# Sparse attention and an ELU feed-forward: staging loads on two queues, halves and pairs of loads, and a new written order

## The chip, the cores and the metric

The kernel runs on one core of a Trainium2 chip. The metric is the device time of one execution in microseconds (us). The kernel before takes 312.54 us (median of 3 runs, 312.42 to 312.94). The core's engines are TensorE (PE, matrix multiplication), VectorE (DVE), ScalarE (ACT, also `exp` and `ln`), GpSimd (POOL) and SyncE (SP). Each has its own instruction queue, worked off in order, and they wait for each other by semaphores. Sixteen DMA engines move data; SP and ACT hand them transfers in one way ("hardware" queues in the profile), POOL in another (the "software" queue, which also converts f32 to bf16 on the way).

## The reference

`q`, `k`, `v` are 8 batches x 8 heads x 576 positions x 64, in f32. The result of attention is 4608 tokens x 512, and goes through two weight matrices:

```python
rel = pos[:, None] - pos[None, :]
mask_local   = (rel >= 0) & (rel < 32)                       # heads 0 to 3
mask_strided = (rel >= 0) & (pos[None] % 32 == pos[:, None] % 32)   # heads 4 to 7
attn = softmax(where(mask, q @ k.T / sqrt(64), -1e9))        # each batch, each head
x = (attn @ v).transpose(0, 2, 1, 3).reshape(4608, 512)
h = x @ w_in                                                 # 512 x 2048
g = where(h > 0, h, exp(min(h, 0)) - 1)
out = g @ w_out                                              # 2048 x 512
```

## The kernel before, in words

**Attention.** The eight heads of a batch are four pairs: `s0`, `s1` (strided, heads 4 to 7) and `l0`, `l1` (local, heads 0 to 3). A pair is two heads of 64 dimensions, side by side on 128 partitions. The positions are split by residue mod 8, so that a strided head has 8 blocks of 72 x 72 scores, of which only the diagonal residues matter. The scores of a pair come in two halves `u` = 0 and 1. For each half: scores on PE (`S`), exp on ACT (`e`), multiplication by a 0/1 mask on DVE (`m`), PE multiplies by `v` and by ones, which gives the sums (`O`), the reciprocal of the sums as ln and exp on ACT (`n`, `r`), and DVE multiplies and writes into `xT` (`x`). `xT` is the transposed activation, 512 x 4608 in bf16.

**Feed-forward.** The tokens are nine chunks of 512. A chunk needs 16 groups (`L`, or its halves `a` and `b` in chunk 0) of four matmuls with `w_in`, ELU on ACT and DVE (`h` exp; `i` on DVE or `j` on ACT clamps; `g` takes the maximum), then four outputs of 16 matmuls with `w_out` (`Z`, each in four parts of four matmuls), a copy out of PSUM (`o` on ACT, `q` on DVE) and a store (`t`). Part `p` of a `Z` needs quarter `p` of `w_out`; group `m` of an `L` needs quarter `m // 4` of `w_in`.

**Loads.** Batches 0 to 2 are transposed on PE (`T`, then a copy by `c` on DVE or `C` on ACT), later batches by DMA transposes (`X`). `load_runs` loads heads of one tensor from POOL (converting), `load_vloc` loads local `v` into `vl`, whose first 32 partitions are then filled by a copy on DVE (`V`, `copy_vloc`, L585); `W` (`copy_vstr`, L588) copies strided `v` into `vs_p` between blocks of ones. Batch 0 starts with the first two strided heads of q and k: four `load_stage` transfers (L287, f32, no conversion) into a staging tile that lies in `g`, half a head's row each, all from SP; casts `K` (DVE) and `k` (ACT), L390, bring them to bf16. At the same time POOL loads the other heads (L232), then `vs`, `ql`, `kl`, `vl` of batch 0, then `w_in` in four quarters (`D.wi0` to `D.wi3`, L266), batch 1, `w_out` in four quarters (`D.wo`, L270) and batch 2.

**What sets the order.** `ORDER` is a written list of tokens. They are issued from the first to the last, each onto its engine's queue, so the list fixes the order on each engine, and nothing reorders it. `w.7.34` at its head issues 34 matmuls of zeros to bank 7. The last number of `T`, `S`, `O`, `L`, `a`, `Z` names PSUM banks (eight in all); a bank can be written again only when its last reader is done. Before the list come the loads and fills of the set-up: the ones between the blocks of `vl` and `vs_p` (`fill_ones`, L314 on DVE, L317 on ACT), zeros at the ends of `kT` (L339 to L341), the identity, and masks by POOL. `F.ms` and `F.ml` make the two masks on DVE.

A place in the order that the prediction needs, that of batch 2's copies `W.2` and `V.2` and what follows them:

```
W.2 T.2s1.k.2 T.2s1.q.1 c.2s1.k T.2s0.q.0 Z.0.3.2.3 c.2s1.q D.qs.3 c.2s0.q V.2 S.2s1.0.01 D.ks.3
S.2s0.0.45 e.2s1.0 T.2l1.k.2 T.2l0.q.6 D.vs.3 c.2l1.k e.2s0.0 T.2l0.k.7 T.2l1.q.0 C.2l0.q c.2l0.k
Z.0.3.3.3 D.ql.3 c.2l1.q L.1.1.7
```

Of the kernel before, what the change touches and what calls it, by code (L numbers as in the profile page):

```python
# [15 lines left out]
S = 576  # L16
D = 64
HG = 4
NS = 8
RS = S // NS  # L20
RP = 80
LQ = 96
LB = S // LQ
# [12 lines left out]
w.7.34 F.ms K.q.0 k.k.0 T.0s0.q.0.0 K.q.1 C.0s0.q.0 T.0s0.k.1.0 k.k.1 c.0s0.k.0 T.0s0.q.0.1  # L36
T.0s1.q.1 c.0s0.q.1 D.wi0.0 S.0s0.0.23 c.0s1.q T.0s1.k.0 e.0s0.0 D.wi1.0 T.0s0.k.1.1 c.0s1.k
c.0s0.k.1 S.0s1.0.67 m.0s0.0 S.0s1.1.45 D.wi2.0 e.0s1.0 S.0s0.1.01 F.ml O.0s0.0.23 e.0s1.1 m.0s1.0
D.wi3.0 T.0l0.q.7 n.0s0.0 m.0s1.1 O.0s1.0.45 e.0s0.1 c.0l0.q D.qs.1 T.0l0.k.6 n.0s1.0 m.0s0.1
O.0s1.1.01 r.0s0.0 c.0l0.k D.ks.1 T.0l1.q.7 r.0s1.0 n.0s1.1 x.0s1.0 r.0s1.1 D.vs.1 T.0l1.k.6 x.0s0.0  # L40
c.0l1.q S.0l0.0.45 C.0l1.k S.0l0.1.23 x.0s1.1 e.0l0.0 O.0s0.1.67 e.0l0.1 D.ql.1 S.0l1.1.01 m.0l0.0
S.0l1.0.45 V.0 n.0s0.1 e.0l1.1 m.0l0.1 O.0l0.0.23 r.0s0.1 m.0l1.1 O.0l0.1.01 n.0l0.0 x.0s0.1 e.0l1.0
O.0l1.1.67 n.0l0.1 m.0l1.0 r.0l0.0 n.0l1.1 O.0l1.0.45 D.kl.1 x.0l0.0 r.0l0.1 r.0l1.1 a.0.0.2 x.0l0.1
n.0l1.0 x.0l1.1 a.0.3.3 r.0l1.0 x.0l1.0 a.0.1.7 D.vl.1 b.0.0 a.0.6.4 h.0.0 b.0.6 i.0.0 g.0.0 b.0.1
h.0.6 D.wo0.0 b.0.3 h.0.1 i.0.6 a.0.9.2 h.0.3 g.0.6 b.0.9 a.0.8.6 i.0.1 h.0.9 b.0.8 i.0.3 i.0.9
a.0.5.4 h.0.8 g.0.1 D.wo1.0 a.0.12.5 a.0.14.0 g.0.9 j.0.8 a.0.2.7 g.0.3 b.0.12 D.wo2.0 g.0.8
T.1s0.q.1 h.0.12 T.1s1.q.3 b.0.5 c.1s0.q c.1s1.q a.0.15.6 h.0.5 i.0.12 D.wo3.0 T.1s0.k.1 b.0.15
# [12 lines left out]
c.2s1.q D.qs.3 c.2s0.q V.2 S.2s1.0.01 D.ks.3 S.2s0.0.45 e.2s1.0 T.2l1.k.2 T.2l0.q.6 D.vs.3 c.2l1.k  # L60
e.2s0.0 T.2l0.k.7 T.2l1.q.0 C.2l0.q c.2l0.k Z.0.3.3.3 D.ql.3 c.2l1.q L.1.1.7 m.2s0.0 o.0.3 X.qs.3
m.2s1.0 O.2s0.0.01 h.1.1 O.2s1.0.23 L.1.5.6 n.2s0.0 i.1.1 g.1.1 L.1.3.4 t.0.3 r.2s0.0 n.2s1.0
x.2s0.0 L.1.11.7 X.ks.3 h.1.3 L.1.7.5 h.1.11 i.1.3 h.1.5 g.1.3 L.1.0.0 h.1.7 D.kl.3 i.1.11 L.1.13.4
i.1.5 r.2s1.0 g.1.11 h.1.0 L.1.6.1 i.1.7 g.1.5 h.1.13 L.1.4.7 h.1.6 i.1.13 g.1.7 j.1.0 L.1.2.6
g.1.13 h.1.4 L.1.15.5 i.1.6 h.1.2 D.vl.3 g.1.0 X.ql.3 j.1.4 L.1.12.4 g.1.6 h.1.15 i.1.2 L.1.10.0
i.1.15 h.1.12 g.1.2 D.qs.4 L.1.8.1 h.1.10 g.1.15 Z.1.0.0.6 g.1.4 h.1.8 x.2s1.0 j.1.12 Z.1.0.1.6
X.kl.3 j.1.8 g.1.12 L.1.14.7 j.1.10 g.1.8 S.2l1.0.45 g.1.10 h.1.14 S.2l1.1.23 D.ks.4 L.1.9.1 e.2l1.1
i.1.14 e.2l1.0 g.1.14 S.2l0.0.23 Z.1.1.0.0 h.1.9 m.2l1.0 m.2l1.1 O.2l1.0.45 i.1.9 Z.1.1.1.0 e.2l0.0
g.1.9 n.2l1.0 O.2l1.1.23 m.2l0.0 Z.1.0.2.6 r.2l1.0 n.2l1.1 Z.1.0.3.6 x.2l1.0 r.2l1.1 O.2l0.0.45
q.1.0 Z.1.1.2.0 n.2l0.0 x.2l1.1 t.1.0 r.2l0.0 S.2s0.1.67 Z.1.1.3.0 e.2s0.1 x.2l0.0 S.2s1.1.12 o.1.1  # L70
S.3s0.1.67 m.2s0.1 S.3s0.0.45 X.qs.4 Z.1.3.0.3 e.2s1.1 e.3s0.0 m.2s1.1 O.2s0.1.12 Z.1.3.1.3 e.3s0.1
m.3s0.0 t.1.1 n.2s0.1 m.3s0.1 O.2s1.1.67 S.2l0.1.45 W.3 Z.1.2.0.0 r.2s0.1 X.ks.4 D.vs.4 e.2l0.1
x.2s0.1 Z.1.2.1.0 n.2s1.1 D.ql.4 m.2l0.1 O.3s0.0.12 O.2l0.1.45 r.2s1.1 Z.1.2.2.0 n.3s0.0 x.2s1.1
Z.1.2.3.0 n.2l0.1 r.3s0.0 O.3s0.1.67 q.1.2 Z.1.3.2.3 r.2l0.1 D.kl.4 x.3s0.0 n.3s0.1 t.1.2 Z.1.3.3.3
x.2l0.1 r.3s0.1 S.3l0.1.12 L.2.5.0 x.3s0.1 e.3l0.1 o.1.3 m.3l0.1 L.2.12.7 h.2.5 t.1.3 i.2.5 L.2.6.6
D.vl.4 h.2.12 g.2.5 X.ql.4 L.2.14.5 i.2.12 h.2.6 g.2.12 j.2.6 L.2.15.0 D.qs.5 h.2.14 g.2.6 L.2.2.7
h.2.15 i.2.14 g.2.14 j.2.15 L.2.1.6 h.2.2 g.2.15 L.2.9.5 D.ks.5 X.kl.4 h.2.1 i.2.2 g.2.2 j.2.1
L.2.3.0 h.2.9 g.2.1 L.2.10.7 h.2.3 i.2.9 g.2.9 j.2.3 L.2.8.6 h.2.10 g.2.3 L.2.4.5 h.2.8 i.2.10
g.2.10 j.2.8 L.2.0.0 h.2.4 g.2.8 L.2.7.7 h.2.0 i.2.4 g.2.4 L.2.13.6 h.2.7 i.2.0 i.2.7 S.3l1.0.45
h.2.13 L.2.11.3 g.2.0 e.3l1.0 g.2.7 S.3s1.1.01 h.2.11 S.3s1.0.45 m.3l1.0 Z.2.0.0.2 X.qs.5 e.3s1.0  # L80
i.2.13 i.2.11 e.3s1.1 O.3l1.0.45 g.2.13 Z.2.0.1.2 n.3l1.0 g.2.11 O.3l0.1.01 r.3l1.0 X.ks.5 m.3s1.1
S.4s0.1.67 m.3s1.0 Z.2.0.2.2 n.3l0.1 x.3l1.0 e.4s0.1 Z.2.0.3.2 r.3l0.1 m.4s0.1 O.3s1.1.67 q.2.0
O.3s1.0.45 n.3s1.1 Z.2.3.0.3 W.4 t.2.0 n.3s1.0 Z.2.3.1.3 x.3l0.1 r.3s1.1 D.vs.5 r.3s1.0 O.4s0.1.01
x.3s1.1 D.ql.5 Z.2.1.0.2 n.4s0.1 x.3s1.0 S.3l0.0.67 r.4s0.1 S.3l1.1.45 Z.2.1.1.2 e.3l0.0 x.4s0.1
e.3l1.1 S.4l1.0.67 m.3l0.0 S.4s0.0.01 Z.2.1.2.2 m.3l1.1 e.4l1.0 D.kl.5 e.4s0.0 O.3l0.0.45 m.4l1.0
O.3l1.1.67 n.3l0.0 m.4s0.0 S.4s1.0.01 Z.2.1.3.2 n.3l1.1 Z.2.3.2.3 r.3l0.0 q.2.1 Z.2.3.3.3 e.4s1.0
x.3l0.0 t.2.1 D.vl.5 r.3l1.1 m.4s1.0 O.4s0.0.45 X.ql.5 S.4s1.1.01 o.2.3 x.3l1.1 Z.2.2.0.2 e.4s1.1
L.3.0.3 D.qs.6 n.4s0.0 m.4s1.1 D.ks.6 t.2.3 L.3.1.0 r.4s0.0 h.3.0 x.4s0.0 L.3.3.1 h.3.1 X.kl.5 i.3.0
L.3.6.4 i.3.1 h.3.3 g.3.0 j.3.3 L.3.11.5 g.3.1 h.3.6 g.3.3 L.3.2.3 h.3.11 i.3.6 L.3.15.1 i.3.11
h.3.2 g.3.6 O.4s1.0.67 g.3.11 h.3.15 L.3.8.0 i.3.2 n.4s1.0 i.3.15 O.4s1.1.45 Z.2.2.1.2 g.3.2 r.4s1.0  # L90
W.5 n.4s1.1 Z.3.0.0.3 g.3.15 r.4s1.1 D.vs.6 Z.2.2.2.2 x.4s1.0 h.3.8 D.ql.6 L.3.4.1 x.4s1.1 j.3.8
X.qs.6 g.3.8 O.4l1.0.45 h.3.4 L.3.10.6 n.4l1.0 i.3.4 L.3.7.0 g.3.4 h.3.10 L.3.14.7 X.ks.6 r.4l1.0
i.3.10 g.3.10 h.3.7 L.3.13.1 x.4l1.0 h.3.14 L.3.9.6 h.3.13 i.3.7 D.kl.6 i.3.14 j.3.13 S.4l0.0.45
g.3.7 Z.2.2.3.2 h.3.9 g.3.13 e.4l0.0 L.3.5.0 i.3.9 o.2.2 g.3.14 Z.3.3.0.4 h.3.5 t.2.2 g.3.9 j.3.5
m.4l0.0 S.4l1.1.12 S.5s0.0.67 L.3.12.5 e.4l1.1 g.3.5 e.5s0.0 m.4l1.1 Z.3.0.1.3 h.3.12 m.5s0.0 i.3.12
# [639 lines left out]
```

## Time and profile before

| what | value |
|---|---|
| time, median of 3 runs | 312.54 us (312.42 to 312.94) |
| the profiled execution's own time | 311.83 us |
| its span | 310.1 us |
| PE busy | 297.5 us, 96% |
| ACT busy, DVE busy | 232.0 us (75%), 225.2 us (73%) |
| POOL busy | 72.1 us (23%) |
| first transposes on PE | 5.51 us |
| first scores on PE, first exp of scores on ACT | 8.60 us, 9.10 us |
| first matmul with `w_in` | 19.66 us |
| end of PE's last matmul | 306.1 us |

The span is the time from the first to the last recorded instruction; the profiled execution's own time is 1.7 us longer than its span, and 0.7 us under the median of the runs. Busy time of PE is the union of its matmuls, so the difference of span and busy time is what PE stands still. Lines such as L608 are lines of the kernel: L608 is the matmul with `w_in`, L642 the matmul with `w_out`. "SPq" is SP issuing a transfer.

### The profile page before, as it was taken

Reading aid. Unit: us, or ns where it says so; the run is one execution under the profiler, and the core shown is the slowest. Engines: PE = TensorE matmul, PEld = TensorE weight load, DVE = VectorE, ACT = ScalarE, POOL = GpSimd, SP = SyncE. Lnnn points to the kernel's source line nnn. Section 1 sums busy time; section 2 is a strip of 40 time slices with the busy share of each in tenths; the row PEclk is TensorE's granted clock in tenths of the full one; section 3 lists DMA queues with packets and bytes.
Section 4 is the critical chain, followed back from the end, with each engine's and each line's share of the span. In section 5 each row is a group of like instructions: output and inputs, shape, how many; then the busy total and the mean of one; then the engine's idle time right before and its main releaser. Section 6 shows DMA issues by size and latency. Waiting matters only on the chain.

```text
span 310.1 us, 6379 instructions
## 1 busy us (share of the span) xinstructions
PE 297.5 (96%) x2379; PEld 152.9 (49%) x2418; DVE 225.2 (73%) x445; ACT 232.0 (75%) x409; POOL 72.1 (23%) x101
## 2 busy tenths in 40 slices
PE   5989999999999999999999999999999999999994
PEld 5855545644554455444544554455444544444443
DVE  4869973789778986997679867995795369984000
ACT  5787966498999999897778899888993768855111
POOL 8723310751084038017210631000000000000000
PEclk9999999999999999999999999999999999999999
DMA  7999999999999999999993699002101220001322
GB/s 147 192 207 205 195 206 225 150 165 151 129 205 185 140 138 183 99 175 174 183 168 86 84 177 157 1 1 70 35 2 34 70 68 0 1 2 35 84 86 68
DMA packets 96392, 36.29 MB, mean 117 GB/s; under 512 B 77706, under 2 KB 91882, under 8 KB 96362
## 3 DMA queue, kind: packets, MB, share of 16 engines
q0 software_dynamic: 64048, 19.40, 61.0%
q1 hardware_dynamic: 32230, 16.42, 28.1%
q8 instruction: 19, 0.31, 0.4%
q14 instruction: 11, 0.09, 0.1%
q10 hardware_dynamic: 84, 0.07, 0.1%
HBM read 39.41 MB, written 9.44 MB: 158 GB/s over the span
## 4 chain that ended last, share of the span: by engine, by line
PE 83%; DMA 7%; ACT 4%; DVE 3%; issue 2%; SPq 0%; ACTq 0%; DVEq 0%
PE ps L608 39%; PE ps L642 33%; DMA vl<-in_v_dram 5%; PE ps L452 3%; PE ps L515 2%; PE ps L522 2%; ACT e L459 2%; DMA g<-in_q_dram 2%; PE ps L668 1%; ACT ln L550 1%; PE ps L406 1%; PE ps L409 1%; ACT ln L556 1%; DVE xT L581 1%; DVE kTl L427 1%
## 5 line engine op out<-in xcount | busy, mean ns | idle before, releaser
L642 PE MATMUL ps<-w_out_sb,g 128*128 128x512 bf16 x539 | 128.4, 379 | 2.1 <-issue 1.4
L608 PE MATMUL ps<-xT,w_in_sb 128*128 128x512 bf16 x558 | 128.2, 380 | 1.6 <-issue 0.6
L616 ACT ACTIVATE he<-ps 128x512 f32<-128x512 f32 x144 | 84.0, 594 | 21.7 <-PE ps L608 19.1
L608 PEld LDWEIGHTS <-w_in_sb 128*128 128x128 bf16 x576 | 54.9, 98 | 65.3 <-issue 1.9
L642 PEld LDWEIGHTS <-g 128*128 128x128 bf16 x560 | 50.7, 98 | 54.9 <-DVE g L634 0.3
L636 DVE TENSOR_TENSOR g<-he,ps 128x512 bf16<-128x512 bf16 x106 | 70.2, 684 | 1.5
L581 DVE TENSOR_TENSOR xT<-ps,ln 64x576 bf16<-64x576 f32 (+1 forms) x64 | 42.3, 677 | 13.3 <-ACT ln L556 11.4
L625 DVE TENSOR_SCALAR he<-he 128x512 bf16<-128x512 f32 x106 | 44.1, 430 | 10.2 <-ACT he L616 9.7
L459 ACT ACTIVATE e<-ps 72x576 bf16<-72x576 f32 (+1 forms) x64 | 39.6, 645 | 8.6 <-PE ps L452 7.1
L550 ACT ACTIVATE ln<-ps 64x576 f32<-64x576 f32 (+1 forms) x64 | 36.7, 585 | 10.0 <-PE ps L479 3.2
L556 ACT ACTIVATE ln<-ln 64x576 f32<-64x576 f32 (+1 forms) x64 | 38.6, 621 | 1.2
L648 ACT COPY osb<-ps 128x512 f32<-128x512 f32 x22 | 12.8, 584 | 24.8 <-PE ps L642 24.7
L634 DVE SCALAR_TENSOR_TENSOR g<-he,ps 128x512 bf16<-128x512 bf16 x38 | 25.8, 683 | 0.7 <-ACT he L623 0.3
L623 ACT ACTIVATE he<-he 128x512 bf16<-128x512 f32 x38 | 23.6, 627 | 1.1 <-DVE g L636 0.3
L472 DVE TENSOR_TENSOR pm<-e,mask_l 128x576 bf16<-128x576 bf16 x32 | 14.3, 456 | 9.6 <-ACT e L459 9.2
L466 DVE TENSOR_TENSOR pm<-e,mask_s 72x576 bf16<-72x576 bf16 x32 | 14.3, 452 | 5.1 <-ACT e L459 4.5
L238 POOL DMA_DIRECT2D ql<-in_q_dram x20 | 16.3, 824 | 6.7 <-DMA qTl<-ql 6.5
L232 POOL DMA_DIRECT2D vs<-in_v_dram x7 | 4.6, 656 | 51.3 <-DVE vsp L588 49.2
L685 DVE COPY osb<-ps 128x128 f32<-128x128 f32 x1 | 0.3, 292 | 22.3 <-ACT osb L684 22.3
L245 POOL DMA_DIRECT2D kl<-in_k_dram x20 | 14.8, 763 | 2.6 <-DMA vs<-in_v_dram 0.9
L255 POOL DMA_DIRECT2D vl<-in_v_dram x8 | 9.4, 1180 | 20.6 <-PE ps L522 12.4
L648 DVE COPY osb<-ps 128x512 f32<-128x512 f32 x13 | 9.0, 691 | 6.6 <-PE ps L642 6.3
(84 smaller groups left out, 177.8 us busy)
## 6 DMA issues: line engine op xcount, KB each, us to landing
out_dram<-osb SPq DMA_DIRECT2D x31, 144.0 KB
vl<-in_v_dram POOLq DMA_DIRECT2D x8, 288.0 KB, 8.5
w_in_sb<-in_moe_w_in_dram POOLq DMA_DIRECT2D x4, 512.0 KB, 12.0
w_out_sb<-in_moe_w_out_dram POOLq DMA_DIRECT2D x4, 512.0 KB, 15.3
vs<-in_v_dram POOLq DMA_DIRECT2D x6, 320.0 KB, 7.1
qs<-in_q_dram POOLq DMA_DIRECT2D x5, 320.0 KB, 12.6
ks<-in_k_dram POOLq DMA_DIRECT2D x5, 320.0 KB, 14.0
ql<-in_q_dram POOLq DMA_DIRECT2D x20, 72.0 KB, 6.2
```

The costliest lines, as they stand in the source:

```text
L459: nc.scalar.activation(e[0:R], tiles.pop(("S", key, u))[0:R], ACT.Exp, scale=scale)
L550: nc.scalar.activation(t, s_ps, ACT.Ln)
L556: nc.scalar.activation(t, t, ACT.Exp, scale=-1.0)
L581: nc.vector.tensor_mul(dst, o_ps, rc)
L608: nc.tensor.matmul(tiles["h", ch, m], lhsT=w_in_sb[:, c, m * 128:(m + 1) * 128], rhs=xT[:, c, ch * CHUNK:(ch + 1) * CHUNK], start=(c == 2) ...
L616: nc.scalar.activation(e, tiles["h", i[0], i[1]], ACT.Exp)
L623: nc.scalar.activation(e1, e, ACT.Relu, bias=1.0, scale=-1.0)
L625: eng.tensor_scalar(e1, e, scalar1=1.0, scalar2=1.0, op0=ALU.min, op1=ALU.subtract)
L634: nc.vector.scalar_tensor_tensor(dst, e1, -1.0, h, op0=ALU.mult, op1=ALU.max)
L636: nc.vector.tensor_tensor(dst, e1, h, op=ALU.max)
L642: nc.tensor.matmul(ops, lhsT=g[ch % 2][:, m, kk * 128:(kk + 1) * 128], rhs=w_out_sb[:, m, :], start=(m == 0), stop=(m == MC - 1), skip_gro ...
L648: eng(o_sb, tiles.pop(("o", int(ch), int(kk))))
```

## The change

- The two k halves of the staging loads are issued by ACT, ahead of its table load; the two q halves stay on SP. All four are cast by ACT except the second q half (`k.k.0 k.q.0 K.q.1 k.k.1`).
- On POOL, the identity and `dist` come first, then `vs` of two heads, `qs`, `ks`, and `vs` of the other two (before: `qs`, `ks`, identity, `dist`, and `vs` of all four).
- `vl` of batch 0 is loaded by two `load_vpair`, each behind the `ql` and `kl` halves of its pair, and copied by two `V.0.0`, `V.0.1`.
- The ones of both `vl` buffers and of `vs_p` are written by memsets on DVE (before: the first `vl` on DVE, the others by copies on ACT). `vs_p` and the zeros of the second `kT` become tokens (`F.vs`, `F.k1`) at the head of the list.
- The first quarter of `w_in` is loaded as two of 256 columns (`D.wi0`, `D.wj0`).
- 28 instead of 34 matmuls of zeros, and the whole list is new. It has the same `S`, `e`, `m`, `O`, `n`, `r`, `x`, `L`, `a`, `b`, `Z`, `h`, `g` and `T` tokens in other places and banks; other counts: `C` 4 to 9 and `c` 22 to 17, `j` 38 to 32 and `i` 106 to 112, `o` 22 to 27 and `q` 13 to 8.

```diff
 ORDER = """
-w.7.34 F.ms K.q.0 k.k.0 T.0s0.q.0.0 K.q.1 C.0s0.q.0 T.0s0.k.1.0 k.k.1 c.0s0.k.0 T.0s0.q.0.1
-T.0s1.q.1 c.0s0.q.1 D.wi0.0 S.0s0.0.23 c.0s1.q T.0s1.k.0 e.0s0.0 D.wi1.0 T.0s0.k.1.1 c.0s1.k
+w.7.28 F.k1 F.vs k.k.0 k.q.0 T.0s0.k.0.0 F.ms C.0s0.k.0 T.0s0.q.1.0 K.q.1 k.k.1 c.0s0.q.0
+T.0s0.k.0.1 S.0s0.0.12 c.0s0.k.1 T.0s0.q.3.1 e.0s0.0 c.0s0.q.1 S.0s0.1.67 m.0s0.0 T.0s1.q.0 e.0s0.1
+O.0s0.0.12 c.0s1.q m.0s0.1 T.0s1.k.7 n.0s0.0 F.ml D.wi0.0 O.0s0.1.56 r.0s0.0 c.0s1.k x.0s0.0 D.wj0.0
+n.0s0.1 S.0s1.0.34 r.0s0.1 T.0l0.q.7 D.wi1.0 e.0s1.0 x.0s0.1 S.0s1.1.01 c.0l0.q T.0l0.k.2 e.0s1.1
...
+S.2s1.0.12 C.2l1.k W.2 T.2s0.q.5 L.1.13.6 e.2s1.0 D.qs.3 c.2s0.q C.2l1.q c.2l0.q T.2s0.k.7 m.2s1.0
+L.1.6.5 h.1.13 D.ks.3 V.2 j.1.13 c.2s0.k L.1.11.4 D.vs.3 h.1.6 g.1.13 D.ql.3 S.2s0.0.23 i.1.6 h.1.11
+S.2l0.1.01 L.1.10.6 g.1.6 e.2s0.0 X.qs.3 i.1.11 e.2l0.1 L.1.8.7 m.2s0.0 h.1.10 g.1.11 O.2s0.0.01
...
+    def load_vpair(b, y):
+        n = HG * LB // 2
+        nc.gpsimd.dma_start(
+            out=blocks(vl_t[b % 2], HG * LB)[PRE:128, y * n:(y + 1) * n],
+            in_=v[b, 2 * y:2 * y + 2].rearrange("h (t p) d -> p (h t) d", p=LQ))
...
-        if nm == "wi":
+        if nm in ("wi", "wj"):
             i = int(what[2])
-            nc.gpsimd.dma_start(out=w_in_sb[:, :, i * 512:(i + 1) * 512],
-                                in_=w_in_v[:, :, i * 512:(i + 1) * 512])
+            f = slice(i * 512, (i + 1) * 512)
+            if i == 0:
+                f = slice(0, 256) if nm == "wi" else slice(256, 512)
+            nc.gpsimd.dma_start(out=w_in_sb[:, :, f], in_=w_in_v[:, :, f])
...
     for u in range(2):
-        load_stage(0, u, q)
-        load_stage(1, u, k)
+        load_stage(nc.sync, 0, u, q)
+        load_stage(nc.scalar, 1, u, k)
     nc.scalar.preload_act_table_set("natural_log_exp_and_others")
-    load_runs("qs", 0, 2, 2)
-    load_runs("ks", 0, 2, 2)
-
     nc.vector.memset(zero, 0.0)
...
     nc.gpsimd.iota(dist, pattern=[[1, RS]], base=RS, channel_multiplier=-1)
+    load_runs("vs", 0, 0, 2)
+    load_runs("qs", 0, 2, 2)
+    load_runs("ks", 0, 2, 2)
+    load_runs("vs", 0, 2, 2)
...
-    fill_ones(vl_t[0], HG * LB)
-    fill_ones(vs_p, HG * NS, nc.scalar.copy)
-    fill_ones(vl_t[1], HG * LB, nc.scalar.copy)
     for t in vl_t:
+        fill_ones(t, HG * LB)
         nc.vector.memset(blocks(t, HG * LB)[0:PRE, 0, :], 0.0)
-    load("vs", 0)
     for y in range(2):
-        for nm in ("ql", "kl"):
-            load_runs(nm, 0, 2 * y, 2)
-    load("vl", 0)
+        load_runs("ql", 0, 2 * y, 2)
+        load_runs("kl", 0, 2 * y, 2)
+        load_vpair(0, y)
+    def fill_kT(t):
+        nc.vector.memset(t["s"][:, NS * RS:KSY], 0.0)
+        nc.vector.memset(t["s"][:, KSY + NS * RS:], 0.0)
+        nc.vector.memset(t["l"][:, 0:PRE], 0.0)
+    fill_kT(kT[0])
...
+        if what == "k1":
+            fill_kT(kT[1])
+        elif what == "vs":
+            fill_ones(vs_p, HG * NS, eng)
...
-    def copy_vloc(b):
+    def copy_vloc(b, y=None):
         t = blocks(vl_t[int(b) % 2], HG * LB)
-        nc.vector.tensor_copy(t[0:PRE, 1:], t[128 - PRE:128, 0:HG * LB - 1])
+        n = HG * LB if y is None else HG * LB // 2
+        i = 0 if y is None else int(y) * n
+        j = max(i, 1)
+        nc.vector.tensor_copy(t[0:PRE, j:i + n], t[128 - PRE:128, j - 1:i + n - 1])
```

## The prediction

> **What bounds the kernel now.** First the page's busy times and its row of slices. PE is the bound, and nearly full:
>
> ```profile
> PE 297.5 (96%) x2379; PEld 152.9 (49%) x2418; DVE 225.2 (73%) x445; ACT 232.0 (75%) x409; POOL 72.1 (23%) x101
> ...
> GB/s 147 192 207 205 195 206 225 150 165 151 129 205 185 140 138 183 99 175 174 183 168 86 84 177 157 1 1 70 35 2 34 70 68 0 1 2 35 84 86 68
> ```
>
> PE stands still for 310.1 - 297.5 = 12.6 us. Some 1.1 us lie before its first instruction and 3.9 us behind its last one. By the table of stretches it is busy for 243.36 of the 246.2 us from 60.0 to 306.2, so 2.8 us are lost there, and some 4.8 us from 1.1 to 60. Only the last two sums can change. The second line shows what rules the first 57 us: slices 2 to 7 (7.75 us each) move about 200 GB/s without a pause. Next the chain that ended last, in order of time:
>
> ```profile
> 1.73 5.03 DMA g<-in_q_dram
> ...
> 40.99 16.29 DMA vl<-in_v_dram
> 57.30 0.69 DVE vl L585
> 58.00 0.37 DVE kTl L427
> 58.58 0.75 DVE kTl L427
> 59.37 1.02 PE ps L608 x4
> ```
>
> The start hangs on the second q half (landed at 6.76). Then the chain goes through a transfer of 16.29 us that is no latency: it stands in a queue of loads. That is batch 2's local `v`, and `V.2` waits for it. The timeline shows both late copies of batch 2, and PE standing still behind them:
>
> ```profile
> 54.80 0.69 DVE L588 COPY vsp<-vs 72x2048 bf16<-72x2048 bf16 x1 [0.94 <-DMA vs<-in_v_dram]
> ...
> 57.30 0.69 DVE L585 COPY vl<-vl 32x1472 bf16<-32x1472 bf16 x1 [0.71 <-DMA vl<-in_v_dram]
> ...
> 59.37 1.02 PE L608 MATMUL ps<-xT,w_in_sb 128*128 128x512 bf16 x4 [0.16 <-DVE kTl L427]
> ```
>
> So the stream of loads ends last at 57 us, whatever the first batch does. POOL's timeline tells when each load lands, because an issue there waits for an earlier load:
>
> ```profile
> 27.27 0.74 POOL L270 DMA_DIRECT2D w_out_sb<-in_moe_w_out_dram  x1 [0.90 <-DMA xT<-in_q_dram]
> 28.94 0.74 POOL L270 DMA_DIRECT2D w_out_sb<-in_moe_w_out_dram  x1 [0.92 <-DMA xT<-in_k_dram]
> ...
> 38.41 0.64 POOL L232 DMA_DIRECT2D vs<-in_v_dram  x1 [2.15 <-DMA w_out_sb<-in_moe_w_out_dram]
> ```
>
> Batch 1's q lands near 27.2, its k near 28.9, the first quarter of `w_out` near 38.3. PE uses them at 27.64, 29.03 and 38.41: within 0.1 to 0.4 us. A head start of PE alone therefore meets one load after another; what counts is how much earlier the stream itself runs. The view of the DMA queues, for 3.0 to 3.5 us:
>
> ```profile
> q0 software_dynamic: 21, 0.02, 76.4%
> q1 hardware_dynamic: 43, 0.03, 18.4%
> ```
>
> 21 packets of POOL's queue take 76.4% of 16 engines: 291 ns each (0.764 x 16 x 500 / 21). From 8 to 9 us it is 212 packets at 124.9%, 94 ns each. POOL's queue starts slowly: 70 packets in all from 3.0 to 4.5 us, and the staging queue gets 79 through beside it, after 291 from 2 to 3 us.
>
> **The change, part by part**, against the profiled execution (311.83 us; the median of the runs is 0.71 above it).
>
> *Staging loads and POOL's order.* SP issues q0, k0, q1, k1 at 0.81, 1.26, 1.73, 2.22 (0.39 to 0.45 each). With two issuers q1 goes at 1.26 and k1 near 1.26, ACT's table load (1.28) ends near 3.0, and its first cast stood at 4.02: hidden. POOL's first load moves from 1.35 to 1.65: the identity's memset ends at 1.15, then 0.30 and 0.20 (rows L302, L305). If the slow start moves with it, it lies at 3.3 to 4.8. The staging queue then has 311 + 0.3 x 291 = 398 packets through by 3.3 and 477 by 4.8, of 704 in all. At 172 per us (5 to 6 us) it is done near 6.1 instead of 7 to 8; q1 and k1 landed at 6.76 and 8.0, and I expect 6.1 to 6.9. POOL's queue has 70 packets by 4.8, 206 by 6.1 (103 per us beside staging) and 586 by 8.0 (200 per us). Before, the views add up to 555 by 8.0. So the stream gains 31 to some 90 packets (the latter with 640 for staging), 0.15 to 0.4 us: I take **-0.3**. Ends: +0.3, if POOL's loads are simply 0.3 us late, and -0.8, if the slow start is gone (1.5 us x 212 - 149 = 169 packets).
>
> *POOL's issues up to `w_in`.* Before, eight (0.76, 0.61, 0.70, four of 0.61, 1.19) with the identity and `dist` between; now ten of about 0.61, as a `vl` half is half of 1.19: 6.05 instead of 5.67. With the two mask fills (0.42, 0.31) `w_in` is issued near 8.45 instead of 8.20, and one issue more follows (0.38 to 0.75). Its first quarter landed near 17.7 from a full queue, so all this is hidden; without that queue it would cost up to 1.0.
>
> *Fills on DVE.* The second `vl` costs 0.70 + 0.09, `vs_p` about 0.93 + 0.09 (1024/768 of 0.698). DVE stood still for 1.78 us at 2.28 waiting for ACT's copy, and the new fills take 1.8 us in that place; `F.ms` ends near 5.2, before q1 lands. Nothing on the path. ACT loses 2.3 us of copies, before it has data. `F.ml` (0.84) now lies ahead of `c.0s1.k` and holds it, and the scores of 0s1, until POOL's masks are done (8.45): at most 0.8 us in batch 0.
>
> *Batch 0.* First scores were 1.84 us behind q1's landing (8.60). Now the two second halves are cast side by side, so 0.62 + 0.3 + 0.4 behind 6.1 to 6.9 gives 7.4 to 8.2, and the first exp moves from 9.10 to about 8.1. From there ACT is the long engine (11.75 us from first exp to last reciprocal, some 11 of it busy). The new order goes depth first (two halves of 0s0 through to `r` before 0s1), so ACT waits for mask and `O` inside. I reckon that batch 0 gives PE 0.3, between -0.5 and +1.2. None of it enters the sum, because the loads end last.
>
> *`V.2`.* Before, PE went on at L.1.1 at 59.37. Now DVE runs `V.2` (57.30, 0.69) and `c.2s0.k` (0.45), and PE goes on with S.2s0.0 at 58.5, less the stream's gain. By counting matmuls (0.216 us for each of 512 columns, 0.2 to 0.4 for scores, transposes and `O`) PE then has 1.1 us more left than at L.1.1 before: 59.6 against 59.37, **+0.2** (0 to 0.5). PE arrives there by itself near 57.7 less batch 0's gain, so the loads bind as long as batch 0 loses less than 0.5. The cover is one `L` (0.86).
>
> *The order behind it.* The matmuls are the same, 0.16 us stand in many places where PE goes from attention to feed-forward, and 2.8 us are lost over 121 such changes in the old list from batch 2's scores on. The new list has 133: 12 x 0.023 = **+0.3**; ends -0.6 (a fifth of the loss gone) and 12 x 0.16 = +1.9. ACT gains five `C` (0.64), five `o` (0.58) and loses six `j` (0.63) and the fills, +0.1 in all; DVE loses 1.3. Neither is full.
>
> *Six matmuls of zeros less*: 6 x 0.112 = 0.67 us before data arrive. PE's small matmuls ran slow before 19.7 us (0.45 for a pair of 288 columns, 0.30 later) in spite of the zeros: 0. The halves of `V.0` (one of 0.55 into two of about 0.3) and of `w_in`: 0.
>
> Sum: -0.3 + 0.2 + 0.3 = +0.2, so 312.0 in the profiled execution and **312.7** on the median.
>
> **The rivals.**
>
> *Faster: the stream gains all of 0.8.* For it: the slow packets stand exactly where staging and POOL's loads start together. Against it: POOL's queue itself was slow, while engines were idle (75% busy). Then `V.2` starts at 56.5; with 0.2 for its place and none for the order, -0.6 to -0.8: 311.8.
>
> *Slower: the fills hold POOL's issues.* The issue of `qs` stood beside DVE's long memset and took 0.762 us, against 0.605 for `ks`. Now three issues stand beside memsets: 3 x 0.16 = 0.5 us eats the gain (+0.7, 313.2); if an issue waited for the whole memset, 0.70 + 0.93 = 1.6 us, less 0.3, come onto the stream: +1.8, 314.3. I take 313.5. It decides once `V.2` starts later than 57.5. [...]
>
> *Slower: the late order.* Each of nine chunks has a new interleaving. For it: 12 more changes, and one `L` as cover for `V.2`. Against it: neither ACT nor DVE gets more work. At half the end, +0.9 for the order, with the rest: 313.4 to 314.
>
> **How the numbers follow.** A median of this kernel can be told from no change at about 0.2% (0.6 us). About as before: 0.37 (312.7; own range 312.0 to 313.2). Faster through the stream or a tighter order: 0.30. Fills 0.13 and late order 0.20: slower 0.33. The range takes 0.8 and a tighter order (-1.4) at one end and the late order's upper half (+1.5) at the other: 311.1 to 314.0.
>
> **What would show it.** Right: first scores near 7.4 to 8.2, batch 1's q landing 0.3 us before 27.2, `V.2` waiting for its load and starting near 57.0, PE still standing there, and 2.5 to 3.5 us lost from 60 to 306. Wrong: `V.2` without a wait, or before 56.5 (faster); POOL issues of over 0.8 us before 6 us and `V.2` behind 57.5 (fills); more than 4 us lost behind 60 us (order).

## The result, and the profile after

The changed kernel takes 311.88 us (median of 16 runs, 310.83 to 312.85); the kernel before takes 312.67 us beside it (16 runs, 311.41 to 314.77). The ratio is 0.9967, with a 95% interval of 0.9951 to 0.9983: about 1.0 us faster (the medians differ by 0.8), more than the 0.2% that can be told from no change. Forecast was 312.7 us. The rival "faster: the stream gains all of 0.8" had 311.8 us.

The profiled execution after took 311.37 us (span 309.4). Busy times from its page:

```profile
PE 297.2 (96%) x2374; PEld 151.6 (49%) x2412; DVE 223.4 (72%) x445; ACT 233.7 (76%) x410; POOL 74.8 (24%) x104
PEclk9559999999999999999999999999999999999999
```

The second line is the granted TensorE clock in tenths, by slices of 7.7 us: half rate in slices 2 and 3. (A 9 at the start of this row does not always mean full rate; experiment 6 comes back to it.) Hold on to the counts in the first: 2,374 matmuls, 2,412 weight loads.

The timeline has the answers to the lines shown of before. Batch 2's two copies and what PE does next:

```profile
54.81 0.68 DVE L603 COPY vsp<-vs 72x2048 bf16<-72x2048 bf16 x1
57.12 0.56 DVE L600 COPY vl<-vl 32x1472 bf16<-32x1472 bf16 x1 [0.54 <-DMA vl<-in_v_dram]
58.10 0.30 PE L464 MATMUL ps<-qTs,kTs 64*128 64x72 bf16 x8
```

`V.2` still waits for its load, and starts 0.18 us earlier than the 57.30 of before. Batch 1's q lands at 27.15, before at 27.27:

```profile
27.15 0.74 POOL L278 DMA_DIRECT2D w_out_sb<-in_moe_w_out_dram  x1 [0.84 <-DMA xT<-in_q_dram]
```

By this pair of traces the stream of loads gained 0.1 to 0.2 us, and the early work much more: first scores at 7.09 instead of 8.60, first `w_in` matmul at 18.38 instead of 19.66. The view of the DMA queues for 4.5 to 5 and for 5 to 6 us says what became of the slow start of POOL's queue (columns: packets, MB, share of 16 engines):

```profile
q0 software_dynamic: 58, 0.06, 73.8%
q0 software_dynamic: 188, 0.18, 117.6%
```

These are nearly its first packets, and they take 102 ns each (0.738 x 16 x 500 / 58), where the first ones of before took 291 ns. They also come later: POOL's queue has 15 packets through by 4.5 us, before 70. But at 5.0 us staging has 694 of its 704 packets through, before 445. So most of POOL's packets now come behind the staging and no longer between its packets, and by 8.0 us the queue has 685 through, before 555.

**A flaw in my reading of before.** The page of before has PE x2379 and PEld x2418. In the full record of e9 (its page is below) matmuls and weight loads are equal in number, 2,412 each; so 39 matmuls were missing from the records of before (38 in the trace after). The groups say which: 558 of 576 matmuls with `w_in` are there, and 21 with `w_out` are missing. Such holes look like standstill of PE, and they made most of my "2.8 us lost behind 60 us over 121 changes". The changed kernel, run once more as a mark (e9, below), left a full record. Its page:

```profile
PE 300.9 (97%) x2412; PEld 152.0 (49%) x2412; DVE 224.0 (72%) x445; ACT 233.6 (75%) x410; POOL 75.0 (24%) x104
```

And its stretches from 60 to 80 and from 80 to 306 us (stretch, length, PE busy and matmuls, granted clock, DMA share, GB/s):

```profile
60.00:80.00 20.00, 20.00 (x152) 1.00 1.65 144
80.00:306.00 226.00, 225.04 (x1539) 1.00 0.73 96
```

Here PE loses 1.0 us behind 60 us. The old list has a full record too, in the kernel before with more matmuls of zeros at its start (e13, below):

```profile
60.00:80.00 20.00, 19.78 (x128) 1.00 1.68 152
80.00:306.00 226.00, 225.53 (x1556) 1.00 0.74 94
```

It loses 0.7 us there, not 2.8. Busy sums of traces with different gaps cannot be compared, so below I mostly compare the times of the same score matmuls, of which no trace misses one.

### The profile page after: what moved, and what is told of

Its sections match the earlier page's. It is cut to its first block, busy times and chain, and to the rows that moved or that the text cites. A ratio compares the mean times of both kernels' runs of the same rounds, so it can differ in the third digit from the quotient of the medians.

```text
span 309.4 us, 6379 instructions
## 1 busy us (share of the span) xinstructions
PE 297.2 (96%) x2374; PEld 151.6 (49%) x2412; DVE 223.4 (72%) x445; ACT 233.7 (76%) x410; POOL 74.8 (24%) x104
## 4 chain that ended last, share of the span: by engine, by line
PE 72%; DVE 15%; DMA 6%; issue 4%; ACT 2%; DVEq 0%; ACTq 0%
PE ps L657 34%; PE ps L623 27%; DVE g L651 6%; DMA vl<-in_v_dram 5%; DVE he L640 5%; PE ps L464 3%; PE ps L527 2%; PE ps L534 2%; DVE xT L593 1%; DMA g<-in_k_dram 1%; DVE g L649 1%; PE ps L683 1%; PE ps L421 1%; PE ps L418 1%; ACT he L631 1%
## 5 line engine op out<-in xcount | busy, mean ns | idle before, releaser
L623 PE MATMUL ps<-xT,w_in_sb 128*128 128x512 bf16 x560 | 129.6, 381 | 1.5 <-DVE g L651 0.4
L651 DVE TENSOR_TENSOR g<-he,ps 128x512 bf16<-128x512 bf16 x112 | 74.0, 681 | 1.5
L640 DVE TENSOR_SCALAR he<-he 128x512 bf16<-128x512 f32 x112 | 46.3, 431 | 16.2 <-ACT he L631 15.7
L471 ACT ACTIVATE e<-ps 128x576 bf16<-128x576 f32 (+1 forms) x64 | 39.4, 646 | 5.8 <-PE ps L464 5.0
L663 ACT COPY osb<-ps 128x512 f32<-128x512 f32 x27 | 15.8, 585 | 29.1 <-PE ps L657 26.1
L232 POOL DMA_DIRECT2D vs<-in_v_dram x8 | 5.3, 662 | 71.7 <-DVE vsp L603 69.4
L649 DVE SCALAR_TENSOR_TENSOR g<-he,ps 128x512 bf16<-128x512 bf16 x32 | 21.7, 680 | 0.6
L638 ACT ACTIVATE he<-he 128x512 bf16<-128x512 f32 x32 | 20.1, 627 | 0.7
L527 PEld LDWEIGHTS <-vsp 72*128 72x128 bf16 x192 | 9.1, 98 | 5.8 <-DVE vsp L603 0.7
L534 PEld LDWEIGHTS <-vl 128*128 128x128 bf16 x144 | 8.2, 97 | 4.4
```

The source lines that it names most:

```text
L471: nc.scalar.activation(e[0:R], tiles.pop(("S", key, u))[0:R], ACT.Exp, scale=scale)
L623: nc.tensor.matmul(tiles["h", ch, m], lhsT=w_in_sb[:, c, m * 128:(m + 1) * 128], rhs=xT[:, c, ch * CHUNK:(ch + 1) * CHUNK], start=(c == 2) ...
L638: nc.scalar.activation(e1, e, ACT.Relu, bias=1.0, scale=-1.0)
L640: eng.tensor_scalar(e1, e, scalar1=1.0, scalar2=1.0, op0=ALU.min, op1=ALU.subtract)
L649: nc.vector.scalar_tensor_tensor(dst, e1, -1.0, h, op0=ALU.mult, op1=ALU.max)
L651: nc.vector.tensor_tensor(dst, e1, h, op=ALU.max)
```

## The experiments

Each ratio is to the kernel before on the same chip, with its 95% interval.

**1. Which half: late order or set-up?** The old list up to batch 2 and the new one behind it, and the reverse:

```diff
 ORDER: <before, up to Z.0.3.3.3 ... c.2l1.q>
+ORDER: <after, all tokens not yet issued>          # e1; e2 is the reverse
```

> The kernel before, with the new list only from L.1.1.7 on (what PE does behind 59.4 us); set-up and everything up to there as before. If the gain of 0.8 to 1.0 us sits in the late order (the traces' work counts say up to 0.45 of it does), this takes 312.2 or less and PE needs about 246.3 instead of 246.7 us from its first matmul of chunk 1 to its last. If the gain is all made before 60 us, it takes 312.5 to 312.9, or a little more for the seam.

> The changed kernel up to the matmuls of L.1.6 (new set-up, new list up to V.2), and from there the old list's remaining tokens. If the gain is made before 60 us, this is as fast as the changed kernel: 0.8 to 1.0 us under before, 311.7 to 311.9. If it is the late order, it stays within 0.4 us of before: 312.3 to 312.7. The seam can cost some tenths in either case.

Measured: 1.0081 [1.0061, 1.0101] and 1.0071 [1.0051, 1.0092]. Both tell nothing about the order. At the seam a PSUM bank is written again before its last reader: in e1 it holds one output of chunk 0 (`Z.0.3`), in e2 two groups of chunk 1 (`L.1.6`, `L.1.13`). So those parts of the computation are left out, and PE loses 3.2 and 1.8 us there alone (16.81 and 18.24 of 20 us busy from 60 to 80). This list can't be cut here, where banks still wait for a reader.

The whole new set-up under the whole old list avoids the seam:

```diff
-w.7.34 F.ms K.q.0 ...          # before's list, in the changed kernel
+w.7.34 F.k1 F.vs F.ms K.q.0 ...
-D.wi0.0 ... V.0
+D.wi0.0 D.wj0.0 ... V.0.0 V.0.1
```

> The new set-up (k halves from ACT, POOL's new order, v by pairs, fills on DVE, first quarter of w_in in two loads) with the old list, to which only the new tokens are added beside the old ones they belong to. If loads bound the first 57 us and the set-up moves them, V.2 starts 0.1 to 0.2 us earlier than 57.30 as in the changed kernel and the time falls by 0.2 to 0.4, to 312.3. If the list makes the gain, nothing: 312.5 to 312.9. First scores near 7.4, since staging lands by 5 to 6.

Measured: 312.00 us, 0.9963 [0.9940, 0.9987], the same as the full change (0.9967). The set-up makes the gain by itself. What the new order adds is too small for these intervals, which are 0.5 and 0.7 us to either side: neither nothing nor the +0.3 us of my sum is excluded. The trace of e3 shows PE ahead of before by 1.0 us in batch 1, and then standing behind `W.2`, whose load had not landed:

```profile
54.90 0.90 DVE L603 COPY vsp<-vs 72x2048 bf16<-72x2048 bf16 x1 [2.25 <-DMA vs<-in_v_dram]
56.94 0.44 PE L464 MATMUL ps<-qTs,kTs 64*128 64x72 bf16 x16 [1.73 <-DVE qTs L435]
```

**2. Does `V.2` hold PE?** Moved behind `g.1.5`, where the next DVE work doesn't need it:

```diff
-L.1.6.5 h.1.13 D.ks.3 V.2 j.1.13 c.2s0.k
+L.1.6.5 h.1.13 D.ks.3 j.1.13 c.2s0.k ... g.1.5 V.2
```

> The changed kernel with V.2 moved on DVE's queue from behind m.2s1.0 to behind g.1.5, some 9 us later; nothing needs it before O.2l1.1. If batch 2's local v still holds PE back at 57 us, as predicted (0.47 and 0.28 us of standstill at 58.1 and 58.8), this takes 0.3 to 0.6 us off the changed kernel: 311.2 to 311.6. If V.2's wait is covered, it changes nothing: 311.7 to 312.0.

Measured: 311.08 us, 0.9942 [0.9911, 0.9972]: 0.8 us under the changed kernel, though the intervals overlap. The same move in the kernel before, and both copies moved under the new set-up with the old list:

> The kernel before, with V.2 moved on DVE's queue behind g.1.5, as the prediction's reading of the chain asks for: PE stood still for V.2's load at 57.3 us. 'The loads end last': PE goes on at 58.0 or earlier instead of 59.4 and 0.7 to 1.3 us go, ratio 0.996 to 0.998. 'PE ends last in the usual run': only the runs with the early clock gain, the median by 0 to 0.5 us, ratio 0.9985 to 1.000.

> The changed set-up with the order of before (which took 0.9963 of the time before), and batch 2's two copies of v moved on DVE's queue behind work that does not need them: W.2 behind the last copy of q and k of batch 2, V.2 behind g.1.5. If the loads of v hold PE through DVE's queue, the stall of 1.73 us at 56.9 us and the 0.9 us ahead of V.2 go: PE is busy for 9.5 us or more from 50 to 60 us instead of 8.05, and the ratio falls to 0.991 to 0.994. If PE would have stood there anyway (its next operands not ready, or the loads behind W.2 late by the move), the ratio stays at 0.995 to 0.998.

Measured: 1.0020 [1.0006, 1.0034] and 0.9994 [0.9970, 1.0017]. Both misses: with the old list the move gains nothing. In e14 PE is busy for 10.00 of 10 us from 50 to 60, as wanted, and then stands behind DVE at 69 us (line below); in e8 it waits for masked scores that DVE has behind `W.2` (0.23 us at 59.85) and for `g` (0.45 us at 68.86). DVE is busy for 8.4 and 9.0 of the 10 us from 60 to 70 in these two traces. That the copy put later delays an ELU instead is what these waits suggest; no run separates it.

```profile
69.02 3.61 PE L608 MATMUL ps<-xT,w_in_sb 128*128 128x512 bf16 x16 [0.28 <-DVE g L636]
```

So taking away the wait at `V.2`, which my whole sum rested on, did not make the kernel before faster.

**3. What takes the slow start of POOL's queue away?** Three kernels: the changed one with one issuer, the changed one with POOL's first loads in their old place, the kernel before with two issuers.

```diff
-    load_stage(nc.scalar, 1, u, k)
+    load_stage(nc.sync, 1, u, k)                  # e5, on the changed kernel
+    load_runs("qs", 0, 2, 2)                      # e6: ahead of the identity again
+    load_runs("ks", 0, 2, 2)
-    load_stage(1, u, k)                           # e7, on the kernel before
+    load_stage(nc.scalar, 1, u, k)
```

> The changed kernel, with all four staging loads issued by SP again (q0, k0, q1, k1); all else as changed. Theory 'two queues': POOL's slow start went because the staging is issued from two queues; then it is back here, POOL's queue has about 555 packets through by 8.0 us (685 in the changed kernel, 555 before), and the ratio to the kernel before rises from 0.997 to 0.999 or more. Rival 'POOL behind': it went because POOL's first load comes 0.25 us later and meets a staging already under way; then some 685 packets stay, and only batch 0 is later by the 0.9 us that the k and q halves' issues take longer: ratio 0.996 to 0.998.

> The changed kernel, with POOL's loads of the second q and k pairs issued ahead of the identity and of the table of distances again, as before the change; the two issuers of the staging stay. 'Two queues': no slow start, some 685 packets of POOL's queue by 8.0 us or a few more, ratio 0.996 to 0.998. 'POOL behind': the slow start returns (291 ns for a packet from 3.0 to 3.5 us, 555 packets by 8.0 us), ratio 0.999 or more.

> The kernel before, with one edit: the k halves of the staging are issued by ACT instead of SP; POOL's order, the fills and the written order stay. 'Two queues': this edit alone takes the slow start away, some 685 packets by 8.0 us instead of 555, and the ratio is 0.996 to 0.998. 'POOL behind': 555 packets, ratio within 0.9985 to 1.0015.

Packets of POOL's queue by 8.0 us: 578 (e5), 715 (e6), 690 (e7), against 555 before and 685 after. The view of the DMA queues of e5, 3.5 to 4 us:

```profile
q0 software_dynamic: 29, 0.03, 99.8%
```

And of e7, 4.5 to 5 us:

```profile
q0 software_dynamic: 59, 0.06, 71.1%
```

275 ns a packet with one issuer, 96 ns with two. The two issuers take the slow start away, alone and in both kernels; with two of them POOL's place doesn't matter. In e7, as in the trace after, POOL's queue has few packets through by 4.5 us (14), and staging has 693 of 704 through by 5.0. The times: e5 314.22 us, 1.0036 [1.0007, 1.0064], so without the second issuer the rest of the change loses; e6 0.9961 [0.9936, 0.9986]; e7 0.9991 [0.9961, 1.0020], a gain too small to see. (In e7's profiled execution PE stood still for 3.0 us at 117.5 us; only its first 60 us are used.)

**4. How much earlier do the loads land?** One trace each is a poor witness. Over all traces with one issuer (before, e1, e5, e13, e14) batch 1's q lands at 27.27, 27.93, 27.62, 27.94, 27.94: mean 27.74. Over the 14 with two issuers and no load added it lands between 26.70 and 27.36, mean 27.09. So the stream gained 0.65 us, and the execution that I had read was the earliest of five. POOL's and PE's timeline of e14, whose first 57 us issue the same work as before:

```profile
26.75 0.75 POOL L270 DMA_DIRECT2D w_out_sb<-in_moe_w_out_dram  x1 [2.37 <-DMA w_in_sb<-in_moe_w_in_dram]
27.94 0.74 POOL L270 DMA_DIRECT2D w_out_sb<-in_moe_w_out_dram  x1 [0.44 <-DMA xT<-in_q_dram]
26.52 1.90 PE L608 MATMUL ps<-xT,w_in_sb 128*128 128x512 bf16 x8 [0.40 <-DMA w_in_sb<-in_moe_w_in_dram]
```

The answer to its first line in the timeline of before:

```profile
25.63 0.74 POOL L270 DMA_DIRECT2D w_out_sb<-in_moe_w_out_dram  x1 [1.89 <-DMA w_in_sb<-in_moe_w_in_dram]
```

The last quarter of `w_in` came 1.1 us later in e14 than in before's trace, and PE stood 0.40 us for it: a wait that the trace of before does not have at all.

At `V.2` the difference is still there. With one issuer and the old order, each trace that leaves `V.2` in its place waits for its load: it starts at 57.30 in before, at 57.59 in e1, and in e13 at

```profile
57.86 0.69 DVE L585 COPY vl<-vl 32x1472 bf16<-32x1472 bf16 x1 [0.71 <-DMA vl<-in_v_dram]
```

With two issuers it waits in the trace after (start at 57.12) and in e15 (56.95); in e3, e6, e7 and e9 it starts at 56.92 to 57.01 without a wait.

**5. Each path made later by itself.** On the changed kernel, beside one more run of it unedited:

```diff
-w.7.28 F.k1 F.vs k.k.0
+w.7.28 F.k1 F.vs f.vs f.vs f.vs k.k.0            # e10: three fills of vs_p on ACT
         load_vpair(0, y)
+    nc.gpsimd.dma_start(out=w_out_sb[:, 0:2, :], in_=w_out_v[:, 0:2, :])   # e11
```

> The changed kernel once more, unedited, as the mark for the three beside it. 0.9967 of the kernel before so far: 0.995 to 0.998 again.

> The changed kernel, with vs_p filled three times more on ACT (1.16 us each as ACT did it before) ahead of the first cast: ACT's first cast moves from 4.82 to about 6.5 us and batch 0 by 1.5 to 1.7 us; no load is touched. My prediction's theory, the loads end last: PE meets the same V.2, at most 0.5 us over the unedited one. New theory, PE itself ends last from batch 0 on: the whole 1.5 us comes out behind (1.2 to 2.2, as the end of the half-rate stretch near 22 us falls), ratio 1.000 to 1.003, and V.2 no longer waits for its load.

> The changed kernel, with a load of 256 KB more in POOL's queue behind batch 0's own loads (two blocks of w_out that are loaded again later): every later load lands some 1.2 us later, batch 0 is untouched. The prediction's theory: V.2 starts near 58.3 and the time is 1.2 us longer, ratio 1.0005. New theory: PE is the bound and the loads have been just in time, so only a part comes out, 0.2 to 0.7 us, ratio 0.997 to 0.999.

| kernel | ratio | first scores | first `w_in` | batch 1's scores | S.2s0.0 | end of PE |
|---|---|---|---|---|---|---|
| e9, unedited | 0.9970 [0.9955, 0.9984] | 7.22 | 18.91 | 32.63 | 58.40 | 305.64 |
| e10, batch 0 late | 1.0082 [1.0054, 1.0110] | +3.05 | +3.68 | +4.79 | +5.11 | +4.21 |
| e11, loads late | 1.0012 [0.9994, 1.0031] | -0.01 | -0.01 | +0.39 | +1.26 | +2.19 |
| e5, one issuer | 1.0036 [1.0007, 1.0064] | +1.20 | +1.23 | +2.18 | +2.20 | +2.16 |

(Times of the profiled executions in us, differences to e9.) The fills of e10 waited for DVE's and ended at 7.8 instead of 6.5 us, so batch 0 was 3.05 us late instead of 1.5 to 1.7. More than that came out at the end: 315.39 against 311.59 us, 3.8 us in the medians, where batch 1's scores were 4.79 us late in the trace. So large a delay can't tell a slack of some tenths from none: my forecast itself let PE bind once batch 0 loses more than 0.5 us. In e11 the loads were late by 1.22 us (batch 1's q at 28.40 against 27.18) and the time by 1.6 us: the loads have no slack, so the new theory's "PE ends last" falls. My forecast's "the loads end last" falls for the changed kernel by the rows of e9 itself, without any delay. DVE's timeline at `V.2` shows it. In e9:

```profile
56.96 0.55 DVE L600 COPY vl<-vl 32x1472 bf16<-32x1472 bf16 x1
```

In e10:

```profile
62.07 0.55 DVE L600 COPY vl<-vl 32x1472 bf16<-32x1472 bf16 x1
```

In e11:

```profile
58.69 0.55 DVE L601 COPY vl<-vl 32x1472 bf16<-32x1472 bf16 x1 [1.04 <-DMA vl<-in_v_dram]
```

In e9 the copy comes 0.16 us earlier than in the profile after, without a wait, and PE is busy for 39.92 of 40 us from 20 to 60: there PE ends last. In the profile after `V.2` waits for 0.54 us, and in e11 for 1.04: there the loads do.

**6. The clock.** In e10 the delay grew by 1.1 us between the first `w_in` matmul and batch 1's scores. Its stretches of 1 us show why (columns: stretch, length, PE busy and matmuls, granted clock, DMA share, GB/s):

```profile
7.00:8.00 1.00, 0.00 (x0) 0.81 1.22 199
24.00:25.00 1.00, 1.00 (x15) 0.50 1.26 203
27.00:28.00 1.00, 1.00 (x3) 0.50 1.24 207
28.00:29.00 1.00, 1.00 (x6) 0.95 1.24 205
```

The `w_in` matmuls ran at half rate until 28.1 us. In the profile after the clock was half from 8.4 to 22.0 us. In e9, the mark, the view says 1.00 throughout, but that is no measurement: where the record of the clock begins late (in before's trace at 20.4 us), the view counts the time ahead of it as full rate. e11 is another such trace, and its matmuls show the half rate:

```profile
22.00:23.00 1.00, 1.00 (x3) 1.00 1.22 202
24.00:25.00 1.00, 1.00 (x7) 1.00 1.24 206
```

Three `w_in` matmuls in the first of these, as in e10 at 0.50, and seven in the second. By such counts (five from 21 to 22 us, then six and seven) e9 ran at half rate until about 22 us. Before's trace did until about 20.4: its first `w_in` matmul, at 19.66, took 0.61 us (0.60 in the trace after at 0.50), the 32 from 20.43 on 7.37 us, 0.23 each. So I gave PE zeros where it stood still, with `V.2` late, then without, then more of them, and the same in the kernel before:

```diff
-w.7.28 ... T.0s0.k.0.0 ... T.0s0.q.1.0 ... T.0s0.q.3.1
+w.7.38 ... T.0s0.k.0.0 w.7.4 ... T.0s0.q.1.0 w.7.9 ... T.0s0.q.3.1 w.7.7
-S.0l1.1.01 ... S.0l1.0.23 ... a.0.0.4
+w.5.4 S.0l1.1.01 ... w.5.8 S.0l1.0.23 ... a.0.0.4 w.5.6
```

> The changed kernel, with V.2 behind g.1.5 (as in the run with V.2 late) and 44 more matmuls of zeros in PE's gaps: 10 ahead of the data, 20 between the first transposes and scores, 18 more, less the gaps' ends, from 16.9 to 19.3 us. The granted clock was 0.5 from 8.4 to 22.0 us, behind a gap of PE from 4.2 to 7 us. If the zeros keep it at 1.0, the first stretch of w_in matmuls at 20.4 runs at 0.216 us each from its start and batch 0 is shorter: 0.8 to 1.3 us less than the unedited one, ratio 0.992 to 0.994. If the clock falls all the same, nothing changes or the zeros delay batch 0: 0.995 to 0.998. [...]

> The changed kernel with the 48 matmuls of zeros alone, V.2 in its place. With V.2 late as well it took 0.9936 of the time before, V.2 late alone 0.9942. If the zeros alone act, 0.994 to 0.9955, and V.2 waits for its load in the profile; if V.2's place made the whole gain, 0.9965 to 0.9975.

> The changed kernel with V.2 late and 64 matmuls of zeros, 16 more where the clock fell at 12.8 us (9 near 9.9, 4 near 11.7, 3 near 12.5 us). If they hold the granted clock at 1.0 through batch 0, the first w_in matmul moves from 18.4 to about 17.8 us and the time falls by 0.3 to 0.6 us more: ratio 0.9915 to 0.993. If the next load (W.2's, landed near 54.4) takes over as the bound or the clock falls all the same: 0.993 to 0.995.

> The kernel before, with 23 more matmuls of zeros in PE's gaps ahead of and in batch 0 (4 behind the first 34, 16 between the first transposes and the second q half, 3 near 18.7 us); no load, no order, no other engine changed. Theory 'the loads end last' (the prediction's): PE's clock is covered by the loads, the ratio is 0.999 to 1.001. Theory 'PE ends last in the usual run': the stretch at half rate, which ended at 20.6 us in the profiled run and later in others, ends earlier or always at the same place; ratio 0.995 to 0.998, with the runs closer together than 1 us.

| kernel | median, us | all runs | ratio |
|---|---|---|---|
| e12, zeros and `V.2` late | 310.83 | 310.36 to 311.11 | 0.9936 [0.9916, 0.9955] |
| e18, the same once more | 311.16 | 310.40 to 311.61 | 0.9934 [0.9909, 0.9959] |
| e15, zeros alone | 311.01 | 310.64 to 312.09 | 0.9948 [0.9931, 0.9964] |
| e16, 16 zeros more, `V.2` late | 311.66 | 310.19 to 312.23 | 0.9958 [0.9940, 0.9976] |
| e13, zeros in the kernel before | 312.93 | 311.53 to 313.78, one 317.35 | 0.9994 [0.9978, 1.0010] |

> The version with V.2 late and 48 matmuls of zeros once more (0.9936, all six runs between 310.4 and 311.1 us): 0.9925 to 0.995 again if the zeros hold; 0.995 to 0.998 if the narrow spread was chance.

e12 (48 zeros; the 44 of its expectation is a slip of addition) beats the kernel before by 0.64 and 0.66% in its two series, the changed kernel by 0.8 us in the series that has both. Its stretches show the half rate cut to 12.5 to 19.3 us:

```profile
12.00:13.00 1.00, 0.73 (x18) 0.74 1.98 160
13.00:19.00 6.00, 5.89 (x94) 0.50 1.39 200
19.00:20.00 1.00, 1.00 (x17) 0.84 1.26 208
```

The zeros alone reach 0.9948 (e15), and `V.2` late alone had 0.9942 (e4): which of the two does more can't be told. More zeros gave the earliest single profile (310.19 us, first `w_in` at 17.53, a clock of 1.00 in each us from 4 on) but no better median; the ratio missed both ranges of its expectation. So a faster clock is not the whole of it. In the kernel before the zeros gained nothing, which is what "the loads end last" said of it. It is a weak test: in e13's trace the half rate still ended at 22.1 us, later than in the trace of before, and the loads were late.

**7. Does the halved first quarter of `w_in` eat the head start?**

```diff
-            if i == 0:
-                f = slice(0, 256) if nm == "wi" else slice(256, 512)
-D.wj0.0
```

> The changed kernel with w_in's first quarter in one load again; all else as changed. POOL's queue then has 514 packets fewer from 8 to 28 us (6,602 in the changed kernel, 6,088 before, for 3.95 and 3.97 MB). If the halves cost the head start of 0.5 us that the queue has at 8 us, batch 1's q lands near 26.8 instead of 27.15 us and the ratio is 0.994 to 0.996; if a half-sized packet takes half the time, nothing moves: landing within 0.2 us of 27.15, ratio 0.996 to 0.998.

Measured: 0.9973 [0.9952, 0.9995], batch 1's q at 27.05; the queue moved 6,098 packets and 3.97 MB from 8 to 28 us, the changed kernel 6,602 and 3.95. The landing did not move: the two loads cost nothing that shows, and they bring nothing that shows.

## Why the prediction was wrong

**The stream, -0.3: the step that failed.** It said "if the slow start moves with it". It did not move, it vanished (e5, e6, e7), which I had kept as the end of the range at -0.8: with two issuers staging is nearly through (694 of 704 packets at 5.0 us) before POOL's queue gets going, so the two hardly interleave. Measured over all traces: -0.65. My argument against this rival, that the queue was slow while engines were idle, proved nothing.

**The late order, +0.3: mis-sized.** Its price, 0.023 us for each of 121 changes, came from 2.8 us of standstill, most of it holes of missing records. With a full record the old list loses 0.7 us there (e13), which is 0.006 for each change, and 12 more of them cost 0.07. e3, with the old order and the same time, agrees, but its interval would allow +0.3 as well. These two terms turned the sign: with -0.65 and about 0 in their places my sum is below zero.

**"None of batch 0 enters the sum, because the loads end last": failed for the changed kernel.** For the kernel before the view holds in each trace that leaves `V.2` in its place (waits of 0.71, 0.64 and 0.71 us in before, e1 and e13). For the changed one it holds in the profile after, and not in e9, where `V.2` doesn't wait. e11 shows that a delay of the loads comes out in full. The two paths meet at `W.2` and `V.2` within a few tenths of a us, and by these traces each execution is ended by whichever is later. What the change brings is both at once: loads 0.65 us earlier and the first `w_in` matmul 0.75 to 1.3 us earlier (18.91 and 18.38 against 19.66). With the sum mended by the first two steps alone, -0.65 + 0.2 + 0 = -0.45 us, the median would be 312.1; measured were -0.8 us against the runs beside it. How the rest divides between batch 0 and `V.2` stays open: e7, which has the loads but only 0.5 us of batch 0, gained 0.3 us with an interval from -1.2 to +0.6.

**`V.2`'s place, +0.2: not confirmed.** S.2s0.0 went at 58.10, as forecast (58.5 less 0.3), but PE lost only 0.34 us from 50 to 60, 0.59 before (with records missing in both); in e9 it lost nothing there.

**Right, or nearly.** First scores 7.09 (7.4 to 8.2 forecast) and second q half at 5.8 (6.1 to 6.9), both a little earlier than forecast; fills on DVE without a cost that shows. The rival "fills hold POOL's issues" didn't come: only the first issue, beside the first long memset, took 0.79 us; those beside the next two took 0.60. No issue waited for a whole memset (the one at 3.57 us took 0.60, `vs_p`'s fill beside it lasted from 3.65 to 4.60), so this trace doesn't show that rival's longer price of 1.6 us. Mis-sized without harm: a `vl` half took 0.88 us to issue, not 0.6, so `w_in` went at 9.21, not 8.45. Batch 1's q landed no later for it (27.15 against 27.27).

## What to carry to other kernels

Compare the count of matmuls with that of weight loads before you price PE's gaps; where they differ (here 2,379 against 2,418), the gaps are partly holes in the record. Where two paths meet within a few tenths of a us, one trace can't say which ends last: take several traces, or delay each path by itself and see what comes out. And look at the clock while data arrive: here PE ran at half rate for 6.8 to 20.5 us in the eleven traces that show it whole, and 48 matmuls of zeros in its gaps took 0.8 us off the changed kernel (with `V.2` late), though nothing off the kernel before.

## What the runs showed of the hardware

**The half-rate stretch lasted 2 to 6 times 3.41 us.** A mean clock of 0.74 in e12's stretch from 12 to 13 us says that it fell at 12.48. Eleven of the 20 traces have both edges on record, in us (3.41 us is half of the shortest stretch):

| kernel | falls at | rises at | between | /3.41 |
|---|---|---|---|---|
| e12, e13, e15, e18 | 12.48, 15.24, 13.72, 12.88 | 19.32, 22.06, 20.54, 19.70 | 6.82 to 6.84 | 2.0 |
| e3 | 8.94 | 19.18 | 10.24 | 3.0 |
| after, e1, e8 | 8.38, 8.48, 7.68 | 22.02, 22.14, 21.32 | 13.64 to 13.66 | 4.0 |
| e5, e17 | 8.26, 7.46 | 25.32, 24.52 | 17.06 | 5.0 |
| e10 | 7.62 | 28.10 | 20.48 | 6.0 |

The lengths are whole multiples of 3.41 us to 0.02 us, and the edges differ between executions (e12 and e18 are the same kernel, 0.4 us apart). With the zeros (e12, e15, e18, and e13 in the kernel before) the clock fell at 12.48 to 15.24 us and stayed low for 6.82 to 6.84; in the seven others it fell at 7.46 to 8.94 and stayed low for 10.24 to 20.48. What sets the two edges, no run here shows: in the profile after PE was busy for 10.80 of 12 us from 9 to 21, with small matmuls, and the clock stayed at half until 22.0, when the dense `w_in` matmuls had run for 1.6 us. By an estimate from the clock of 0.50 and these lengths, 3.41 us more of half rate under those costs half of that, 1.7 us of PE's time. In eight of the other traces (before, e9 and e11 among them) the record begins late (in before at 20.4 us), so the start of their half rate is not known. In e16 the clock is 1.00 in each us from 4 to 29, and from 8.59 us on a pair of matmuls of 288 columns took 0.29 to 0.31 us, against 0.44 to 0.45 in the trace after at 0.50 (19.34 and 19.82 us).

**POOL's queue starts slowly beside staging from one queue, not from two**: 275 and 291 ns for its first packets (e5, before) against 96 and 102 (e7, after). With one queue the two interleave from 3 to 7 us (staging 445 of 704 packets through at 5.0 us in before, 556 in e5); with two, staging is nearly through at 5.0 us (694 in after, 693 in e7) and most of POOL's packets follow it. Why they are slow beside the one queue, no run here shows.
